# Which engine multiplies the keys by the running products: VectorE for all units in place of GpSimd from the second on

## The chip, the cores and the metric

One core of a Trainium2 chip runs the whole kernel. The metric is device microseconds from start to end of one execution; the median of the runs is what counts. A profiled execution stands beside them, with the time of every instruction of every engine.

## The reference

The kernel computes a linear attention with a state, and then two dense feed-forward layers on its output. For 32 heads (4 batches x 8) of 768 steps, with vectors of 40 elements:

```python
for t in range(S):
    y[:, :, t] = np.einsum('bhd,bhde->bhe', rt, state)
    Sa = np.einsum('bhde,bhe->bhd', state, at)
    state_decay = state * wt[:, :, None, :] - np.einsum('bhd,bhe->bhde', Sa, bt)
    state = state_decay + np.einsum('bhd,bhe->bhde', vt, kt)
```

The 3072 x 320 result goes through h = x @ w_in, a smooth ramp, g @ w_out (320 to 2048 to 320), and a second layer of the same size whose nonlinearity is s * relu(h)^2 + b. The weights of both layers come as float64.

## The kernel before, in words

**The attention** is cut into 24 chunks of 32 steps, and two chunks make a unit: 12 units. Within a chunk the decays w become running products. `prep_a` (line 428) makes what a unit needs before the state is known:

- `products_from_right` (L375) scans suf, the running products from the right end of each chunk, and `products_from_left` (L383 a reciprocal, L384 a scan) makes pre, those from the left. Both are VectorE, and both scan in place.
- L445 multiplies ekb (the k and b vectors, 104 x 1024 elements for each of two) by suf. The last one sets the flag kbm, and `stage_k` sends ekb to the tile tk, part of it through DRAM.
- L454 multiplies XA (the a vectors, four instructions of 40 x 512 elements) by pre. XA is a ring of four chunks, and `loads_a` refills a chunk's place after TensorE has used it for xp.
- L466 multiplies XA and ekb on TensorE into ap; L473 (ScalarE) and L474 (VectorE) copy it to am, and SyncE writes am to DRAM (a_scr). Then L484 (VectorE) puts the masked half back into XA by transposes.

`inverse` (line 547) reads a_scr back as la, and inverts triangles of 16 x 16 in steps on VectorE: L566 makes tmp, L569 subtracts it from ln, each step needing the one before. The result goes to DRAM (l_scr). `mend` loads it as lt and completes it to 32 x 32 on TensorE (L598 pl, L609 pq). `chain_a` and `chain_s` then carry the state from chunk to chunk (xp L709, up L724, sp L747, and on VectorE xr = sp x pc, L759), and `chain_b` makes the output of a chunk (tq, tp, gg, py), with the mask of gg on VectorE (L827).

**The first layer** works on 256 tokens (one unit) at a time, as soon as they are there: fin (L954), a nonlinearity on ScalarE and VectorE (`post`, L919 to L922), a split of g into a high and a low part (L932 on ScalarE, L934 on GpSimd), and fout (L985). What isn't done beside the attention is done after it. The second layer (L964, L1003) comes last and works on 512 tokens at a time. GpSimd also converts weights (L238, L327, L330; the first layer's early, the second's after the attention) and clears tiles (L313).

**The order of the work** is not left to a compiler. Each of the functions named is a generator that yields operations with an engine and an estimated duration, and waits for flags or buffers. `Order.run` (line 146) simulates them as threads: it gives each engine the operation that can begin first, the due time (`DUE`, `STEP`) deciding among those close to each other, and issues the instructions in that order. Each engine then runs its instructions strictly in the order issued, with semaphores between engines. The durations it counts with are:

```python
def dve(n, fn, also=False, two=False):
    return Op("DVE", 70 + n / 0.96, fn, also=also, port=two)
...
def pool(n, fn, also=False, rate=2.1):
    return Op("POOL", 150 + n * rate, fn, 170, also=also, port=n > 16)
```

An operation with `port` set can't be planned beside another one with it; `dve2` is `dve` with `two` set. So the order is planned with 2300 ns for an ekb multiplication on GpSimd and 1137 ns on VectorE, and 1225 ns and 603 ns for one of xa.

Buffers that hold a unit's suf, pre and ekb (es, ew, ekb) are single, and am takes the place of pre; so the next unit's pre is loaded when L484 has read am.

Of the kernel before, what the change touches and what calls it, by code (L numbers as in the profile page):

```python
# [33 lines left out]
NS = 8  # L34
FIRST = 300
LOAD = 0.5
LIGHT = 1
SOON = 0
HOT, LEAD = -59.0, 100

# [157 lines left out]
def pe(dur, fn, share=0.0, spare=False):  # L198

    op = Op("PE", dur, fn, 197)  # L200
    op.small, op.share, op.spare = share > 0, share or 0.95, spare
    return op


def dve(n, fn, also=False, two=False):

    return Op("DVE", 70 + n / 0.96, fn, also=also, port=two)
# [6 lines left out]
def act(n, fn, also=False, more=0):  # L214
    return Op("ACT", 60 + n / 1.2 + more, fn, also=also)
# [6 lines left out]
def dma(nbytes, fn, count=1, flag=None, each=475):  # L222

    op = Op("SP", each * count, fn, 980, flag, nbytes / 360)
    op.count = count
    return op
# [22 lines left out]
def fast_path(ctx, tc, inside, ws_em, wp_em, a_em, kb_em, v_em, r_em, v_tok, eye, mask_a, mask_g, eye_kb,  # L249
              w1_in, w1_out, w2_in, w2_out, sb, out):  # L250
    nc = tc.nc
# [117 lines left out]
    def products_from_right(suf):  # L369

        back = lambda t: flat(t)[:, ::-1]
        for h in range(0, 2 * NP, NS):
            a = slice(h, min(h + NS, 2 * NP))
            n = a.stop - h
            yield dve2(2 * n * 33, lambda: nc.vector.tensor_tensor_scan(out=back(suf[:, a]), data0=back(suf[:, a]), data1=back(start_s[:, 0:n]), initial=1.0,  # L375
                                                                    op0=ALU.mult, op1=ALU.add), h > 0)

    def products_from_left(suf, pre):

        for h in range(0, 2 * NP, NS):  # L380
            a = slice(h, min(h + NS, 2 * NP))
            n = a.stop - h
            yield dve(50, lambda: nc.vector.reciprocal(out=start_p[:, 0:n, 0], in_=suf[:, a, 0]))  # L383
            yield dve2(2 * n * 32, lambda: nc.vector.tensor_tensor_scan(out=flat(pre[:, a]), data0=flat(pre[:, a]), data1=flat(start_p[:, 0:n]), initial=0.0,  # L384
                                                                    op0=ALU.mult, op1=ALU.add))
# [42 lines left out]
    def prep_a():  # L428
        for u in range(NU):
            yield due("prep", u)  # L430
            mk, eng = (dve2, nc.vector) if u < 1 else (pool, nc.gpsimd)
            yield Wait(("start", 1))
            yield Wait(("lw", u + 1))
            suf = sufs[u]
            yield from products_from_right(suf)
            yield act(32, lambda: nc.scalar.copy(out=pc[:, :, 2 * u % 6:2 * u % 6 + 2], in_=suf[:, :, 0].rearrange("p (a c) -> p a c", c=2)))
            yield Wait(("lp", u + 1))
            pre = pres[u]
            yield from products_from_left(suf, pre)
            od.set("pc", 2 * u + 2)  # L440
            od.spawn(stage_e(u, suf, pre), due("stage", u).value)
            yield Wait(("lk", u + 1))
            ekb = ekbs[u]
            for x in range(2):
                yield mk(1024, lambda: eng.tensor_tensor(out=ekb[:, x], in0=ekb[:, x], in1=suf[:, :, 1:C + 1], op=ALU.mult), x > 0)  # L445
            od.set("kbm", u + 1)
            od.spawn(stage_k(u, ekb), due("stage", u).value)
            for c2 in range(2):
                yield Wait(("la", 2 * u + c2 + 1))
                for x in range(2):  # L450
                    r = slice(64 * x, 64 * x + 40)
                    xa = XA[(2 * u + c2) % RING]
                    mk, eng = (pool, nc.gpsimd) if u >= LIGHT else (dve2, nc.vector)
                    yield mk(512, lambda: eng.tensor_tensor(  # L454
                        out=xa[r, x], in0=xa[r, x], in1=pre[r].rearrange("e (p c) t -> e c p t", c=2)[:, c2], op=ALU.mult), x > 0)
            kbv = ekb.rearrange("e y (p c) t -> e c p y t", c=2)
            for c2 in range(2):
                yield Acq("a")
                ap = pa.tile([128, 8, 2, C], F32, tag="a", name="ap")
                xa = XA[(2 * u + c2) % RING]  # L460

                def mm():
                    for m in range(8):
                        for q in range(4):
                            p, x = 8 * (q // 2) + m, q % 2
                            nc.tensor.matmul(ap[32 * q:32 * q + 32, m], lhsT=xa[64 * x:64 * x + 40, x, p, :],  # L466
                                             rhs=kbv[64 * x:64 * x + 40, c2, p], start=True, stop=True, tile_position=(64 * x, 32 * q))

                yield pe(1030, mm, 0.17)
                if c2 == 0:  # L470
                    yield Wait(("ew", u + 1), ("const", 1))
                    am = emp.tile([128, 2, 2, 8, C], F32, tag="ew", name="am")
                yield act(256, lambda: nc.scalar.copy(out=am[:, 1, c2], in_=ap[:, :, 1, :]))  # L473
                yield dve(256, lambda: nc.vector.tensor_tensor(  # L474
                    out=am[:, 0, c2], in0=ap[:, :, 0, :], in1=mska.unsqueeze(1).to_broadcast([128, 8, C]), op=ALU.mult), True)
                od.rel("a")
                if c2 == 1:
                    od.set("ekb", u + 1)
                yield dma(128 * 2048, lambda: nc.sync.dma_start(
                    out=a_scr[u][c2].rearrange("m q t j -> (q t) m j"), in_=am[:, 1, c2]), 1, ("A", 2 * u + c2 + 1))  # L480
            for c2 in range(2):
                for q in range(4):
                    d0 = 0 if q % 2 else 64
                    yield dve(256, lambda: nc.vector.transpose(out=XA[(2 * u + c2) % RING][d0:d0 + 32, q % 2, 8 * (q // 2):8 * (q // 2) + 8, :],  # L484
                                                               in_=am[32 * q:32 * q + 32, 0, c2]), q > 0)
                od.set("XL", 2 * u + c2 + 1)
            od.rel("ew")

    def stage_e(u, suf, pre):

        def put():
            for x in range(2):
                nc.sync.dma_start(out=em_scr[u][x].rearrange("b e n -> e b n"), in_=pre[64 * x:64 * x + 32].rearrange("e (b a) t -> e b (a t)", b=4))
                nc.sync.dma_start(out=et_scr[u][x].rearrange("p e n -> e p n"), in_=pre[64 * x + 32:64 * x + 40].rearrange("e (p c) t -> e p (c t)", c=2))

        yield dma(128 * 3072, put, 4, ("et", u + 1))
        yield Acq("tk")
        tk = att.tile([128, NP, 2, C], F32, tag="tk", name="tk")
        tks[u] = tk, att.tile([128, 4, 2, C], F32, tag="tb", name="tb")
        for i, t in enumerate((pre, suf[:, :, 0:C])):  # L500
            yield act(1176, lambda: nc.scalar.activation(out=tk[0:104].rearrange("p a c t -> p (a c) t"), in_=t, func=AF.Abs,
                                                         accum_out=tot[0:104, 2 * u + i:2 * u + i + 1]))
            if i == 0:
                od.set("ew", u + 1)
        od.set("tot", u + 1)
        yield Wait(("kbm", u + 1))
        od.rel("es")

    def stage_k(u, ekb):

        yield Wait(("tot", u + 1))
        tk, tb = tks[u]

        def put():
            for x in range(2):
                for y in range(2):
                    g = 2 * (1 - x) + y
                    nc.sync.dma_start(out=tk[32 * g:32 * g + 32].rearrange("e p c t -> e (p c t)"), in_=ekb[64 * x:64 * x + 32, y].rearrange("e a t -> e (a t)"))

        def tail():  # L520
            for x in range(2):
                nc.sync.dma_start(out=kt_scr[u][1 - x].rearrange("y h e n -> e (y h) n"),
                                  in_=ekb[64 * x + 32:64 * x + 40].rearrange("e y (h a) t -> e (y h) (a t)", h=4))

        yield dma(128 * 1024, tail, 2, ("kt", u + 1))
        yield dma(128 * 4096, put, 4, ("tk", u + 0.5), 650)
        yield Wait(("kt", u + 1))
        yield dma(128 * 1024, lambda: nc.sync.dma_start(out=tb.rearrange("p i c t -> p (i c t)"), in_=kt_scr[u].rearrange("x y h e n -> (x y h e) n")), 1, ("tk", u + 1))
        yield Wait(("ekb", u + 1), ("tk", u + 1))
        od.rel("ekb")  # L530
# [710 lines left out]
```

## Time and profile before

| | us |
|---|---|
| median of 3 runs | 1236.17 |
| lowest and highest | 1234.88, 1250.49 |
| profiled execution, its own time | 1242.7 |
| its span, first to last instruction | 1240.9 |

Rows name a line (L445), an engine, an operation, and tiles as output<-inputs. The engines are PE (TensorE), PEld (its weight loads), DVE (VectorE), ACT (ScalarE), POOL (GpSimd) and SP (SyncE). A granted clock of 1.00 is TensorE's full 2.4 GHz, 0.50 is 1.2 GHz. The chain of waits follows the work that ended last back to the start, each piece being what released the next; what isn't in it was done early enough.

### The profile page before, as it was taken

The page shows a single profiled execution, that of the slowest core. Times are in us where ns is not written, and L with a number is a line of the kernel's source. Part 1 is how long each engine was busy: PE and PEld are TensorE (multiplying, and loading weights), DVE is VectorE, ACT ScalarE, POOL GpSimd, SP SyncE. Part 2 cuts the span into 40 slices and gives each one's busy share as a digit, 9 for nine tenths or more (in the row PEclk, how much of TensorE's full clock was granted, in tenths as well). Part 3 has the DMA queues.
Part 4 walks back from the last instruction along what each step waited for, and adds up shares of the span by engine and source line. Part 5 has one row for each costly group of instructions (what it writes and reads, how often), then busy time and mean ns, then how long its engine had stood idle before and what let it go on. Part 6 is the DMA issues. An engine that isn't in the chain of part 4 may idle for free.

```text
span 1240.9 us, 47386 instructions
## 1 busy us (share of the span) xinstructions
PE 1125.5 (91%) x20654; PEld 1025.2 (83%) x20654; DVE 736.5 (59%) x1629; ACT 757.4 (61%) x1537; POOL 360.9 (29%) x333
## 2 busy tenths in 40 slices
PE   3897899889898989989899999999999999999995
PEld 3796788778787778878788889999888889888895
DVE  4775877666568676777647343277974344444432
ACT  2433767557476565765666677688765555555553
POOL 5555563414143331323421112366540000000000
PEclk9898699899899988989999999999999999999998
DMA  7875525464555546474432210156201010101000
GB/s 195 239 199 138 125 58 124 91 140 99 110 108 109 124 95 126 81 149 104 96 79 61 44 43 14 34 172 205 69 1 48 1 47 4 45 10 26 16 7 24
DMA packets 188415, 107.36 MB, mean 87 GB/s; under 512 B 149126, under 2 KB 167686, under 8 KB 186950
## 3 DMA queue, kind: packets, MB, share of 16 engines
q1 hardware_dynamic: 188198, 104.24, 35.4%
q8 instruction: 164, 2.69, 0.9%
q14 instruction: 53, 0.43, 0.1%
HBM read 78.25 MB, written 19.66 MB: 79 GB/s over the span
## 4 chain that ended last, share of the span: by engine, by line
PE 72%; DVE 8%; ACT 5%; issue 5%; DMA 5%; SPq 1%; POOL 1%; DVEq 0%; ACTq 0%; POOLq 0%
PE h L954 14%; PE h L964 12%; PE acc L985 12%; PE acc L1003 12%; PE h L1034 6%; PE gg L819 2%; PE sp L747 2%; PE tq L768 2%; PE ap L466 2%; PE py L840 1%; PE xp L709 1%; PE up L724 1%; DMA lt<-lscr 1%; PE tp L802 1%; PE ptx L873 1%
## 5 line engine op out<-in xcount | busy, mean ns | idle before, releaser
L934 POOL TENSOR_TENSOR gl<-g,gh 128x512 fp32r<-128x512 f32 x96 | 125.4, 1306 | 433.9 <-ACT gh L932 380.0
L954 PE MATMUL h<-xh,w 128*128 128x256 f32 x1152 | 228.1, 301 | 5.7 <-DVE g L922 2.9
L954 PEld LDWEIGHTS h<-xh,w 128*128 128x128 f32 x1152 | 182.2, 198 | 12.4 <-issue 3.9
L985 PE MATMUL acc<-w,gh 128*128 128x320 f32 x768 | 190.6, 335 | 0.0
L1003 PE MATMUL acc<-w,gh 128*128 128x320 f32 x768 | 173.1, 312 | 2.6 <-ACT o L1016 2.1
L932 ACT CAST gh<-g 128x512 fp32r<-128x512 f32 x192 | 118.9, 619 | 61.1 <-DVE g L922 37.1
L1003 PEld LDWEIGHTS acc<-w,gh 128*128 128x128 f32 x768 | 132.2, 189 | 11.6 <-ACT o L1016 3.9
L934 DVE TENSOR_TENSOR gl<-g,gh 128x512 fp32r<-128x512 f32 x96 | 68.1, 709 | 117.7 <-ACT gh L932 117.5
L985 PEld LDWEIGHTS acc<-w,gh 128*128 128x128 f32 x768 | 130.9, 198 | 5.0 <-issue 0.2
L985 PE MATMUL acc<-w,gl 128*128 128x320 f32 x384 | 123.0, 320 | 0.0
L1003 PE MATMUL acc<-w,gl 128*128 128x320 f32 x384 | 118.7, 309 | 0.0
L928 ACT ACTIVATE g<-g,sbt 128x512 f32<-128x512 f32 x96 | 78.3, 816 | 64.8 <-DVE g L926 64.7
L954 PE MATMUL h<-xl,w 128*128 128x256 f32 x384 | 111.5, 290 | 0.4 <-issue 0.4
L922 DVE SCALAR_TENSOR_TENSOR g<-h,g 128x512 f32<-128x512 f32 x96 | 66.1, 688 | 75.1 <-ACT h L921 46.4
L919 ACT ACTIVATE g<-h,sbt 128x512 f32<-128x512 f32 x96 | 65.9, 687 | 64.8 <-PE h L954 61.7
L926 DVE SCALAR_TENSOR_TENSOR g<-h,g 128x512 f32<-128x512 f32 x96 | 66.3, 691 | 60.7 <-ACT g L925 60.6
L925 ACT ACTIVATE g<-h 128x512 f32<-128x512 f32 x96 | 57.2, 596 | 72.1 <-PE h L964 72.1
L1034 PE MATMUL h<-w 128*128 128x256 f32 x668 | 91.5, 299 | 0.0
L1034 PEld LDWEIGHTS h<-w 128*128 128x128 f32 x668 | 87.1, 204 | 1.4 <-issue 0.3
L238 POOL TENSOR_TENSOR t<-t,w 128x384 int32<-128x384 int32 x64 | 67.6, 1060 | 68.3 <-DVE t L236 41.0
L759 DVE TENSOR_TENSOR xr<-sp,pc 40x320 f32<-40x320 f32 x92 | 44.8, 487 | 58.4 <-PE sp L747 56.9
L964 PE MATMUL h<-xx,w 128*128 128x512 f32 x288 | 76.8, 402 | 2.1 <-DVE w L330 2.1
(107 smaller groups left out, 2277.7 us busy)
## 6 DMA issues: line engine op xcount, KB each, us to landing
w<-in_w_in SPq DMA_DIRECT2D x32, 384.0 KB
w<-in_w_out SPq DMA_DIRECT2D x32, 320.0 KB
ekb<-in_kb_em SPq DMA_DIRECT2D x12, 832.0 KB
tk<-ekb SPq DMA_DIRECT2D x48, 128.0 KB
suf<-in_ws_em SPq DMA_DIRECT2D x12, 429.0 KB
pre<-in_wp_em SPq DMA_DIRECT2D x12, 416.0 KB
xa<-in_a_em SPq DMA_DIRECT2D x48, 80.0 KB
xr<-in_v_tok SPq DMA_DIRECT2D x48, 80.0 KB
```

The source lines that it names most:

```text
L238: (pool, n, lambda: nc.gpsimd.tensor_tensor(out=t, in0=t, in1=lo, op=ALU.add)),
L919: yield act(512, lambda: nc.scalar.activation(out=g, in_=h, func=AF.Relu, bias=sbt[:, 2:3]), more=93)
L922: yield dve(512, lambda: nc.vector.scalar_tensor_tensor(out=g, in0=h, scalar=1.0, in1=g, op0=ALU.subtract, op1=ALU.add))
L926: yield dve(512, lambda: nc.vector.scalar_tensor_tensor(out=g, in0=h, scalar=0.0, in1=g, op0=ALU.max, op1=ALU.mult))
L928: yield act(512, lambda: nc.scalar.activation(out=g, in_=g, func=AF.Identity, scale=sbt[:, 0:1], bias=sbt[:, 1:2]), more=230)
L932: yield act(512, lambda: nc.scalar.copy(out=gh, in_=g))
L934: yield mk(512, lambda: eng.tensor_tensor(out=gl, in0=g, in1=gh.bitcast(F32), op=ALU.subtract))
L954: yield pe(8 * 118, lambda: [nc.tensor.matmul(h[:, i, :], lhsT=a, rhs=b, start=m == 0, stop=m == 7) for m, (a, b) in enumerate(mm)])
L964: yield pe(4 * 224, lambda: [nc.tensor.matmul(h, lhsT=a, rhs=b, start=4 * i + m == 0, stop=4 * i + m == 7) for m, (a, b) in enumerate(mm[4 ...
L985: yield pe(6 * 147, lambda: [nc.tensor.matmul(acc[0, n][u], lhsT=a, rhs=b, start=p == 0 and m == 0, stop=p == NFF // 2 - 1 and m == 5) for ...
L1003: yield pe(3 * 147, lambda: [nc.tensor.matmul(acc[1, n][u], lhsT=a, rhs=b, start=f == 0 and m == 0, stop=f == NFF - 1 and m == 2) for m, ( ...
L1034: yield pe(2 * 109, lambda: [nc.tensor.matmul(h[:, i, :], lhsT=wh[:, 0:128], rhs=wh[:, 0:256], start=True, stop=True) for i in range(2)], ...
```

## The change

In `prep_a` the engine of the multiplications at L445 (ekb by suf) and L454 (xa by pre) is VectorE for all 12 units, where GpSimd did them from the second unit on. The constant LIGHT, the first unit on GpSimd, falls away. The planner counts with VectorE's durations for them.

```diff
-LIGHT = 1
...
     def prep_a():
         for u in range(NU):
             yield due("prep", u)
-            mk, eng = (dve2, nc.vector) if u < 1 else (pool, nc.gpsimd)
+            mk, eng = dve2, nc.vector
             yield Wait(("start", 1))
...
                     xa = XA[(2 * u + c2) % RING]
-                    mk, eng = (pool, nc.gpsimd) if u >= LIGHT else (dve2, nc.vector)
+                    mk, eng = dve2, nc.vector
                     yield mk(512, lambda: eng.tensor_tensor(
```

## Rows read from the trace of the kernel before

**Rows 1.** The page, busy time (share of the span), and the chain by engine.
```profile
PE 1125.5 (91%) x20654; PEld 1025.2 (83%) x20654; DVE 736.5 (59%) x1629; ACT 757.4 (61%) x1537; POOL 360.9 (29%) x333
...
PE 72%; DVE 8%; ACT 5%; issue 5%; DMA 5%; SPq 1%; POOL 1%; DVEq 0%; ACTq 0%; POOLq 0%
```

**Rows 2.** Windows: length, busy us (instructions) of each engine, granted clock, DMA.
```profile
55.00:640.00 585.00, 517.64 (x14138) 468.24 (x14138) 409.46 (x1021) 350.28 (x781) 227.03 (x189) 0.90 0.52 115
...
100.00:200.00 100.00, 83.58 (x2376) 74.89 (x2376) 67.67 (x167) 64.33 (x152) 56.95 (x55) 0.81 0.47 103
400.00:500.00 100.00, 89.42 (x2685) 79.52 (x2689) 65.38 (x173) 57.74 (x129) 27.94 (x24) 0.86 0.54 115
1000.00:1100.00 100.00, 99.71 (x558) 89.53 (x557) 41.44 (x68) 57.92 (x95) 0.00 (x0) 1.00 0.10 25
```

**Rows 3.** The chain of waits in order of time: start us, us, what.
```profile
214.70 6.70 DMA lt<-lscr
...
397.46 2.13 DVE tmp L566
...
513.03 2.00 DVE ln L569
515.03 2.62 DVE pre L384
...
555.00 1.86 DVE tmp L566
561.05 2.02 DVE ln L569
...
594.72 2.42 DMA lt<-lscr
...
606.35 1.95 DVE ln L569
```

**Rows 4.** The tile ekb: ns shortest/median/longest, first and last start.
```profile
L445 POOL TENSOR_TENSOR ekb<-ekb,suf x22: 2152/2189/2661, 58.5 to 613.6; 104x1024 f32<-104x1024 f32 x22
...
L445 DVE TENSOR_TENSOR ekb<-ekb,suf x2: 1211/1624/2037, 15.0 to 17.0; 104x1024 f32<-104x1024 f32 x2
```

**Rows 5.** The tile xa, the same view.
```profile
L454 POOL TENSOR_TENSOR xa<-xa,pre x44: 1255/1276/1302, 64.2 to 632.5; 40x512 f32<-40x512 f32 x44
...
L454 DVE TENSOR_TENSOR xa<-xa,pre x4: 673/682/690, 18.1 to 20.7; 40x512 f32<-40x512 f32 x4
```

**Rows 6.** The tiles ln and pre, the same view.
```profile
L566 DVE TENSOR_TENSOR tmp<-ln,la x180: 135/241/2134, 53.4 to 676.6; 128x15 f32<-128x15 f32 x24, 128x28 f32<-128x28 f32 x24, 128x39 f32<-128x39 f32 x24, 128x48 f32<-128x48 f32 x24
L569 DVE TENSOR_TENSOR ln<-ln,tmp x180: 140/207/2124, 54.8 to 677.2; 128x15 f32<-128x15 f32 x24, 128x28 f32<-128x28 f32 x24, 128x39 f32<-128x39 f32 x24, 128x48 f32<-128x48 f32 x24
...
L384 DVE TENSOR_TENSOR_SCAN pre<-pre,start_p x48: 650/685/2719, 7.8 to 610.2; 104x256 f32<-104x256 f32 x48
```

**Rows 7.** Windows of multiplications on GpSimd: length, VectorE busy (instructions), clock, DMA.
```profile
224.46:228.77 4.31, 1.44 (x2) 0.50 0.67 87
301.70:305.67 3.97, 0.98 (x2) 1.00 0.62 142
512.75:517.10 4.35, 4.35 (x4) 1.00 0.02 4
```

**Rows 8.** The timeline of VectorE: start us, us, instruction [idle before <-releaser].
```profile
58.99 2.12 DVE L569 TENSOR_TENSOR ln<-ln,tmp 128x39 f32<-128x39 f32 x1
...
304.08 0.99 DVE L759 TENSOR_TENSOR xr<-sp,pc 40x320 f32<-40x320 f32 x2 [6.54 <-PE sp L747]
...
512.95 2.08 DVE L569 TENSOR_TENSOR ln<-ln,tmp 128x64 f32<-128x64 f32 x1
514.96 2.70 DVE L384 TENSOR_TENSOR_SCAN pre<-pre,start_p 104x256 f32<-104x256 f32 x1
...
606.28 2.02 DVE L569 TENSOR_TENSOR ln<-ln,tmp 128x28 f32<-128x28 f32 x1
```

**Rows 9.** Waits on GpSimd: us in total, times, longest.
```profile
POOL xa L454 <- DMA xa<-in_a_em: 7.7, 4, 2.9
```

## The prediction

> **What bounds the kernel now.** I read the page first, then the windows, the chain of waits, and at last the views of the two tiles. On the page TensorE is busy 91% of the span, VectorE 59%, GpSimd 29%, and TensorE holds 72% of the chain that ended last, VectorE 8%, GpSimd 1% [rows 1]. The reader is to see that this average hides two stages. From 1000 to 1100 us TensorE is busy 99.71 of 100 us at a granted clock of 1.00: the second MoE layer is pure TensorE work and nothing in this change touches it. From 55 to 640 us, where the attention units 1 to 11 are prepared and carried through, it is busy 517.64 of 585 us, so 67 us are idle, and the mean granted clock is 0.90; VectorE is busy 409.46 us (70%) and GpSimd 227.03 us (39%) [rows 2]. The end moves only by what the change does to those 67 idle us and to the clock there: matmul work is the same, and what isn't done beside the attention is done after it.
>
> The chain of waits in that stage says what makes TensorE wait. Four times it stands on the landing of lt, the triangular inverse on its way back from DRAM (16.6 us in all; first and last piece shown), and in other places it runs through VectorE's scans of pre and the steps of the inverse (tmp and ln) [rows 3]. Neither L445 nor L454 on GpSimd holds a single piece of the chain between 55 and 660 us. So the multiplications are hidden as durations; what can be felt is how they stand in VectorE's way.
>
> **What the change removes.** GpSimd loses 22 ekb instructions of 2189 ns (median) and 44 xa instructions of 1276 ns [rows 4, 5]: 48.2 + 56.1 = 104 us, 9.5 us for each of 11 units. GpSimd has idle time anyway, so that gives nothing by itself. But six pieces of the chain are VectorE instructions that ran much longer than usual: 2.13, 2.00, 2.62, 1.86, 2.02 and 1.95 us [rows 3], where a step of the inverse has a median of 241 or 207 ns and a scan one of 685 ns [rows 6]. Each lies in the shade of an ekb multiplication; the instruction at 512.95 us (2.08 us) and the one at 514.96 us (2.70 us) show it, as the two ekb multiplications run from 512.75 us for 4.35 us [rows 7, 8]. Such an instruction counts as busy but stands until GpSimd is done. I went through VectorE's timeline for all 22 + 44 multiplications and took the usual duration off each VectorE instruction beside them: 16 are stretched by ekb, 28.0 us in all, and 11 by xa, 8.0 us; the first is the one of 2.12 us at 58.99 us, the last large one that of 2.02 us at 606.28 us [rows 8]. So 36 us of VectorE's busy time go. On the chain, the six pieces sum to 12.6 us; at usual durations (five steps at about 0.2, one scan at 0.69) they would take 1.7 us, so 10.9 us go there.
>
> VectorE instructions that read PSUM aren't stretched: the pair of L759 at 304.08 us, inside three xa multiplications that run from 301.70 us for 3.97 us, took 0.99 us, 0.5 us each [rows 7, 8]. These ran beside GpSimd and will stand behind VectorE's own multiplications: the change takes away a lock on some instructions and puts a queue in front of all.
>
> The Trainium skill, page "SBUF — State Buffer", section "SBUF: two separate sides", has this as a rule: a GpSimd instruction and a VectorE instruction with two SBUF inputs (or in a two-port mode) exclude each other for the whole instruction, whichever started first. By that rule all 104 us are closed to such instructions, and if VectorE had always had one ready, the change would take 104 us off and not 36. The trace agrees with the mechanism (2.70 us against 0.69), but in the windows of the multiplications VectorE was busy from 4.35 of 4.35 us down to 1.44 of 4.31 [rows 7], so the 36 us counted are used.
>
> **What it adds.** VectorE gets the 22 ekb and 44 xa instructions. Unit 0 runs them there already: ekb took 1.21 us at the least and 1.62 us in the median of two, of which one was held up; xa 0.68 us [rows 4, 5]. So 22 x 1.21 to 1.62 = 26.6 to 35.7 us, and 44 x 0.682 = 30.0 us: 57 to 66 us, 5.1 to 6 us for each unit. The spread stays because GpSimd keeps some 120 us in the stage (227 - 104), beside which the new instructions may be held up in turn. I take 61 us.
>
> It also moves waits. On GpSimd xa waited four times for its DMA, 7.7 us in all, the longest 2.9 us [rows 9]. GpSimd could afford this; on VectorE, which issues in order, everything behind waits too: steps of the inverse, xr = sp x pc for the chain, the masks of gg. Bounds: 0, if the hand-made order puts xa where the load has landed, and 7.7 us or more, if it doesn't. I take 7.7 us. No DMA is added or removed, but the ones behind kbm and XL (tk, kt, am to DRAM) are issued from SyncE's queue at other times.
>
> **The sum.** VectorE: +61 + 7.7 - 36 = +33 us in 585, three us for each unit, so that its busy share goes from 70% to 75%. How much reaches the end? On the page VectorE holds 8% of the span's chain and is busy 59%: about one us in seven counts (0.135). That gives +4.4 us. The second way goes by pieces: -10.9 us; 6 of the 22 ekb were felt before, and if as many are felt at 1.21 to 1.62 us that is +7 to +10; xa and its waits at 0.135 of 37.7 us is +5.1. Together +1 to +4. I take +4.
>
> The preparation itself gets shorter: 2 x 2.19 + 4 x 1.28 = 9.5 us become 2 x 1.42 + 4 x 0.68 = 5.6 us. Bounds: nothing, as no piece of the chain is one of these multiplications, and the 16.6 us that the chain stands on lt, if an earlier xa brings an earlier inverse. The loop from xa over ap, A and inverse to lt goes through four transfers and the thirty steps of an inverse, and one piece on lt alone is up to 6.70 us [rows 3]; so I take nothing.
>
> Last, the order. Every engine's order is written by the list scheduler in Order.run, with 2300 and 1225 ns for the two GpSimd instructions and 1137 and 603 ns on VectorE. With other costs on another engine the whole order from unit 1 on is another one. Its price has no row; the nearest is the clock: 0.81 from 100 to 200 us, 0.86 from 400 to 500, 0.90 over the stage [rows 2]. A stretch of 100 us at 0.81 and not 0.90 costs 9 us of TensorE's time, one at 0.90 and not 0.81 gives that back. I take +1 and keep 9 us either way for the range. In all +5 us: by the profiled execution's own time, 1242.7 us, 1247.7; the median of the runs shown is 6.5 us under it, so 1236.2 + 5 = **1241 us**, no difference that a measurement of this kernel could tell from none (it can tell about 2%, 25 us).
>
> **The rivals.**
> *VectorE becomes the bound of the attention stage (slower).* Place: the inverse of unit u, thirty dependent steps on VectorE, between which the list scheduler puts whatever else is ready, now six multiplications of unit u + 1. For it: the inverse is what lt waits for, and the inverse's steps and scans are VectorE's pieces on the chain. Against: VectorE idles 175 us of the 585. It decides if the added time is felt in full, not at one in seven: +33 us, 1269 us; above 0.75 felt it is 25 us and past 2%.
> *The lock goes and the stage tightens (faster).* For it: six stretched pieces on the chain, 10.9 us, and 16.6 us of waits for lt; if VectorE's idle time takes in the new work, both go: -27 us, 1209 us. Against: these waits have their length from DMA and from the order as well, and other waits come late next.
> *All of it lies beside TensorE's work.* Neither lock nor added work is felt: 1236 us. For it: 86% of the chain isn't VectorE's or GpSimd's. Against: the six pieces.
> The Trainium skill, page "Perfetto Trace Analysis", section "Optimizing Scalar/DVE Operations", warns that moving operations between these two engines might not help, as they share a port; that would be this last case, and the stretched rows are what speaks against it being all.
>
> **How the numbers follow.** Chances: the forecast 0.48, with a range of its own of 1226 to 1257 (the clock's 9 us and the bounds of the DMA wait and of ekb); the slower rival 0.27, the faster one 0.13, no effect 0.12. The range goes from 1214, near the faster rival, to 1272, the slower one with 3 us beyond its price; under and over it lie about 0.1 each. Faster by over 2% means under 1211.5 us: most of the faster rival at its full price, 0.09. Slower by over 2% means over 1260.9 us: most of the slower rival, 0.24. The rest is 0.67.
>
> **What would show it.** Right: no GpSimd row for L445 and L454; VectorE ekb near 1.2 to 1.6 us x24 and xa near 0.68 us x48; the maximum of scans and of inverse steps down from 2.7 and 2.1 us to that of other GpSimd instructions (about 1.3 us); VectorE busy some 20 to 30 us more; TensorE busy from 55 to 640 us within 10 us of before. Wrong: the units run closer together or further apart by over 2 us each, with more or less time on lt in the chain, or a granted clock in the stage that is off 0.90 by over 0.03.

## The result, and the profile after

The changed kernel takes 1221.26 us (median of 12 runs, 1217.52 to 1231.22); the kernel before took 1238.76 us beside it (12 runs). The ratio is 0.985, with an interval of 0.983 to 0.988: faster by 1.5%, some 18 us. The forecast was slower by 5 us; its own range, 1226 to 1257 us, misses the result, the wide one (1214 to 1272) holds it. The profiled execution took 1219.44 us with a span of 1217.6, so the two profiles differ by 23 us, 6 us more than the medians. The ratios are formed from the faster runs of both kernels (those over 1.5% above a kernel's fastest are left out), so they can differ a little from the quotient of medians. Lines stand one lower than before (L445 is L444), as LIGHT is gone.

The page of the changed kernel: busy time, and the filler matmuls that TensorE runs until the first layer can begin; the third line is the one of the fillers before:

```profile
PE 1106.8 (91%) x20532; PEld 1003.7 (82%) x20532; DVE 763.6 (63%) x1695; ACT 757.3 (62%) x1537; POOL 265.2 (22%) x267
...
L1033 PE MATMUL h<-w 128*128 128x256 f32 x546 | 79.4, 309 | 0.0
...
L1034 PE MATMUL h<-w 128*128 128x256 f32 x668 | 91.5, 299 | 0.0
```

Beside [rows 1]: VectorE has 27 us more, GpSimd 96 us less. TensorE has 19 us less. 12 us of it are fillers: the first layer's first block begins at 146.4 us and not at 162.0. The other 7 us are the same 19986 matmuls done in less time, at a mean granted clock of 0.954 for 0.943 over the span. TensorE's idle time falls by 5 us (110.8 for 115.4). As fillers stand where TensorE would wait, some 17 of the 23 us are waiting that went, and 7 are matmuls that ran faster.

The window of the attention stage, columns as in [rows 2]:

```profile
55.00:640.00 585.00, 523.25 (x14775) 468.64 (x14775) 452.09 (x1125) 368.33 (x819) 133.24 (x128) 0.92 0.54 118
```

In the same 585 us TensorE now issues 14775 matmuls, 637 more, at a clock of 0.92 for 0.90. The stage as a whole has moved forward: more of everybody's work falls into the window, VectorE's too.

The tiles ekb, xa, ln and pre of the changed kernel, beside [rows 4 to 6]:

```profile
L444 DVE TENSOR_TENSOR ekb<-ekb,suf x24: 1208/1217/2315, 15.0 to 598.9; 104x1024 f32<-104x1024 f32 x24
...
L453 DVE TENSOR_TENSOR xa<-xa,pre x48: 672/689/1746, 18.1 to 621.5; 40x512 f32<-40x512 f32 x48
...
L565 DVE TENSOR_TENSOR tmp<-ln,la x180: 127/240/1389, 53.4 to 650.2; 128x15 f32<-128x15 f32 x24, 128x28 f32<-128x28 f32 x24, 128x39 f32<-128x39 f32 x24, 128x48 f32<-128x48 f32 x24
L568 DVE TENSOR_TENSOR ln<-ln,tmp x180: 132/207/1285, 54.6 to 650.5; 128x15 f32<-128x15 f32 x24, 128x28 f32<-128x28 f32 x24, 128x39 f32<-128x39 f32 x24, 128x48 f32<-128x48 f32 x24
...
L383 DVE TENSOR_TENSOR_SCAN pre<-pre,start_p x48: 671/686/1367, 7.8 to 596.9; 104x256 f32<-104x256 f32 x48
```

The median durations are those that unit 0 had before. The longest step of the inverse falls from 2.1 to 1.3 or 1.4 us, the longest scan from 2.7 to 1.4. A *hold* is here the time for which a VectorE instruction stands, counted as busy, while one of GpSimd runs. What is left are holds by GpSimd's other instructions: the longest step, 1.39 us at 606.53 us, stands beside one of gl (L933) that runs from 606.51 us for 1.29. The last step of the last inverse starts at 650.5 us and not at 677.2.

The timeline shows the start of it. In the kernel before, VectorE at the end of the first inverse, and GpSimd (POOL) beside it:

```profile
94.03 0.69 DVE L384 TENSOR_TENSOR_SCAN pre<-pre,start_p 104x256 f32<-104x256 f32 x1 [4.22 <-DMA w<-in_w_in]
...
97.15 2.11 DVE L569 TENSOR_TENSOR ln<-ln,tmp 128x15 f32<-128x15 f32 x1
...
96.56 5.12 POOL L445 TENSOR_TENSOR ekb<-ekb,suf 104x1024 f32<-104x1024 f32 x2
```

and in the changed kernel:

```profile
86.54 0.90 DVE L568 TENSOR_TENSOR ln<-ln,tmp 128x15 f32<-128x15 f32 x1
...
87.69 0.68 DVE L383 TENSOR_TENSOR_SCAN pre<-pre,start_p 104x256 f32<-104x256 f32 x1
```

The last step of the inverse starts at 86.54 us and not at 97.15. Two things are to be seen. That step took 2.11 us beside two ekb multiplications of unit 2; a step takes some 0.2 us in the median. And a scan of unit 2, for which VectorE stood idle for 4.22 us, lay in the middle of the inverse before; now it comes behind the inverse's end: the order of issue is another one. (The profile names a load of weights as what the scan waited for; the load of its own data was issued only at 89.66 us.) So there are two candidates, the hold and the order, and the experiments part them.

### The profile page after: what moved, and what is told of

Its sections match the earlier page's. It is cut to its first block, busy times and chain, and to the rows that moved or that the text cites. A ratio compares the mean times of both kernels' runs of the same rounds, so it can differ in the third digit from the quotient of the medians.

```text
span 1217.6 us, 47095 instructions
## 1 busy us (share of the span) xinstructions
PE 1106.8 (91%) x20532; PEld 1003.7 (82%) x20532; DVE 763.6 (63%) x1695; ACT 757.3 (62%) x1537; POOL 265.2 (22%) x267
## 5 line engine op out<-in xcount | busy, mean ns | idle before, releaser
L933 POOL TENSOR_TENSOR gl<-g,gh 128x512 fp32r<-128x512 f32 x96 | 129.6, 1350 | 524.9 <-ACT gh L931 490.9
L953 PE MATMUL h<-xh,w 128*128 128x256 f32 x1152 | 222.8, 296 | 5.9 <-DVE g L921 3.8
L953 PEld LDWEIGHTS h<-xh,w 128*128 128x128 f32 x1152 | 177.4, 192 | 10.2 <-DVE g L921 4.2
L933 DVE TENSOR_TENSOR gl<-g,gh 128x512 fp32r<-128x512 f32 x96 | 66.8, 696 | 122.1 <-ACT gh L931 121.9
L1002 PEld LDWEIGHTS acc<-w,gh 128*128 128x128 f32 x768 | 131.7, 188 | 11.1 <-ACT o L1015 3.1
L984 PEld LDWEIGHTS acc<-w,gh 128*128 128x128 f32 x768 | 128.6, 195 | 8.1 <-issue 3.0
L237 POOL TENSOR_TENSOR t<-t,w 128x384 int32<-128x384 int32 x64 | 70.3, 1102 | 71.6 <-DVE t L235 43.9
L1033 PE MATMUL h<-w 128*128 128x256 f32 x546 | 79.4, 309 | 0.0
L1033 PEld LDWEIGHTS h<-w 128*128 128x128 f32 x546 | 75.4, 215 | 1.3 <-issue 0.3
L953 PEld LDWEIGHTS h<-xl,w 128*128 128x128 f32 x384 | 74.2, 193 | 2.3 <-issue 2.0
```

Source lines behind the costliest of these rows:

```text
L237: (pool, n, lambda: nc.gpsimd.tensor_tensor(out=t, in0=t, in1=lo, op=ALU.add)),
L933: yield mk(512, lambda: eng.tensor_tensor(out=gl, in0=g, in1=gh.bitcast(F32), op=ALU.subtract))
L953: yield pe(8 * 118, lambda: [nc.tensor.matmul(h[:, i, :], lhsT=a, rhs=b, start=m == 0, stop=m == 7) for m, (a, b) in enumerate(mm)])
L984: yield pe(6 * 147, lambda: [nc.tensor.matmul(acc[0, n][u], lhsT=a, rhs=b, start=p == 0 and m == 0, stop=p == NFF // 2 - 1 and m == 5) for ...
L1002: yield pe(3 * 147, lambda: [nc.tensor.matmul(acc[1, n][u], lhsT=a, rhs=b, start=f == 0 and m == 0, stop=f == NFF - 1 and m == 2) for m, ( ...
L1033: yield pe(2 * 109, lambda: [nc.tensor.matmul(h[:, i, :], lhsT=wh[:, 0:128], rhs=wh[:, 0:256], start=True, stop=True) for i in range(2)], ...
```

## The experiments

The runs were on several chips, and the kernel before ran beside each with medians from 1233.31 to 1245.46 us; so ratios to the kernel before of the same chip are compared, with intervals of some 0.003 to 0.007 either way.

### Engine and order, one at a time

The planner's word for an operation (`pool`, `dve2`) sets the order, the engine in the instruction sets who does it. So each can be changed alone.

```diff
  order_before_on_dve
-            mk, eng = (dve2, nc.vector) if u < 1 else (pool, nc.gpsimd)
+            mk, eng = (dve2, nc.vector) if u < 1 else (pool, nc.vector)
  order_after_on_pool
-            mk, eng = (dve2, nc.vector) if u < 1 else (pool, nc.gpsimd)
+            mk, eng = (dve2, nc.vector) if u < 1 else (dve2, nc.gpsimd)
```

and the same for xa.

> The order of issue is that of the kernel before (the planner counts GpSimd's engine and durations for the multiplications from unit 1 on), but VectorE executes them. Theory A, the lock: what the change gave (17.5 us, ratio 0.985) comes from GpSimd no longer holding up VectorE, so most of it is here, 10 to 18 us under before. Theory B, the order: it comes from the planner's new order, so this is within 4 us of before, or slower by up to 10 us, since VectorE gets 5 us more of each unit at places that weren't planned for it.

Measured: 0.989 (0.983 to 0.995), which is 13.8 us of that chip's 1244.59; the medians themselves are 9.5 us apart.

> The order of issue is that of the changed kernel (the planner counts VectorE's durations and VectorE as the engine), but GpSimd executes the multiplications from unit 1 on. Theory A, the lock: the stretched steps come back, so the time is that of before or above, 0 to +15 us. Theory B, the order: 10 to 18 us under before, as in the changed kernel.

Measured: 0.992 (0.989 to 0.996). Neither theory stands alone: the engine gives 1.1% in the old order, the new order 0.8% with GpSimd still at work. From there to the changed kernel (0.985) the engine gives 0.7% in the new order. The order gives 0.4% with VectorE, which the intervals don't tell from nothing.

What the engine does is seen in the tile ln of order_after_on_pool, beside the one of the changed kernel above, whose order it has:

```profile
L566 DVE TENSOR_TENSOR tmp<-ln,la x180: 130/242/2229, 52.9 to 663.9; 128x15 f32<-128x15 f32 x24, 128x28 f32<-128x28 f32 x24, 128x39 f32<-128x39 f32 x24, 128x48 f32<-128x48 f32 x24
L569 DVE TENSOR_TENSOR ln<-ln,tmp x180: 123/212/5205, 53.6 to 664.1; 128x15 f32<-128x15 f32 x24, 128x28 f32<-128x28 f32 x24, 128x39 f32<-128x39 f32 x24, 128x48 f32<-128x48 f32 x24
```

The long steps are back, and the last one starts at 664.1 us for 650.5.

### One of the two, and one of the units

ekb_only and xa_only take one of the two lines of the diff; unit1_only has `u < 2` for ekb and LIGHT = 2; all_but_unit1 has GpSimd for `u == 1` alone.

> Only the 22 ekb multiplications go to VectorE, planned and executed there; xa stays on GpSimd. Theory A, the lock: ekb carried 28 of the 36 us of stretching and all six stretched pieces of the chain, so this gives most, 9 to 15 us under before. Rival, the latency of the preparation: xa stands last before ap, and its four multiplications are 5.1 of the 9.5 us; then ekb alone gives half or less, 3 to 8 us.

> Only the 44 xa multiplications go to VectorE, planned and executed there; ekb stays on GpSimd. Theory A, the lock: 8 of 36 us of stretching, so 0 to 5 us under before. Rival, the latency: 8 to 14 us under before. If both single moves and neither theory fit (both give all, or neither gives any), the order as such is what moves the time.

Measured: ekb_only 0.990 (0.986 to 0.994), 15 us by the medians; xa_only 0.999 (0.995 to 1.002). That is as the holds were counted (28 us of stretching for ekb, 8 for xa) and against the latency of the preparation as the reason. But each of the two edits also writes an order of its own, so alone they don't show it.

> Both multiplications go to VectorE for unit 1 alone (with unit 0, as before); units 2 to 11 keep GpSimd. Theory S, the start: in the changed kernel the first inverse ends 11 us earlier (86 for 97 us) and the first layer's first block starts 16 us earlier, so unit 1 alone gives 8 to 15 us and the rest adds little. Rival, every unit: the gain is one of 1 to 2 us for each unit, so unit 1 alone gives 0 to 3 us.

> The other half: unit 1 keeps GpSimd, units 2 to 11 go to VectorE. Theory S, the start: 0 to 5 us under before. Rival, every unit: 12 to 17 us under before.

Measured: unit1_only 0.999 (0.995 to 1.002), all_but_unit1 1.002 (0.998 to 1.006). Both theories are wrong: neither part gives anything, and together they give 1.5%. unit1_only does have the early start, with 592 fillers for 668, and loses it again on the way. So parts don't add up, as is to be expected if each edit rewrites the order from the second unit to the last; the next runs test that.

### How much an order is worth

```diff
  planned_as_measured (GpSimd)
-                yield mk(1024, lambda: eng.tensor_tensor(out=ekb[:, x], ...
+                yield Op("POOL", 2189, lambda: eng.tensor_tensor(out=ekb[:, x], ...
  after_as_measured (VectorE)
-                yield mk(1024, lambda: eng.tensor_tensor(out=ekb[:, x], ...
+                yield Op("DVE", 1217, lambda: eng.tensor_tensor(out=ekb[:, x], ...
```

and so for xa; after_less and after_more have other numbers in the second.

> A control: GpSimd executes all, as in the kernel before, and only the planner's durations for the two are set to what the trace shows (2189 for 2300 ns, 1276 for 1225 ns). Nothing that a theory speaks of is changed. If the order as such is worth little, this is within 4 us of before; if any small change of the plan moves the time by some 10 us, it is off by that, either way, and then gains of that size in single runs say little of their cause.

Measured: 0.993 (0.989 to 0.996). Some 4 to 5% on two planned durations, no engine changed, and the kernel is faster by 0.7%.

> A control on the changed kernel: VectorE executes all, and only the planner's durations for the two are set to what the trace of the changed kernel shows (1217 for 1137 ns, 689 for 603 ns). If the order of the changed kernel is one among many, this falls anywhere from 0.980 to 1.000 of before; if VectorE as the engine is what makes the order good, it stays at 0.982 to 0.989.

Measured: 0.975 (0.969 to 0.980), 1214.18 us beside 1245.46: clear of the changed kernel's 0.985. A truer plan could be the reason, so the error was made larger (1057 and 517 ns) and turned around (1297 and 775 ns):

> The changed kernel with the planner's durations set as far below its own as after_as_measured has them above (1057 and 517 ns; its own are 1137 and 603, the trace shows 1217 and 689). If a truer plan is what made after_as_measured faster, this is slower than the changed kernel, 0.990 to 1.000 of before. If orders differ by luck, it is anywhere from 0.975 to 1.000.

> The changed kernel with the planner's durations above those of the trace (1297 and 775 ns). If a truer plan is what counts, or one with some room, this stays near after_as_measured, 0.972 to 0.982 of before; if luck, anywhere from 0.975 to 1.000.

Measured: after_less 0.977 (0.972 to 0.982), after_more 0.993 (0.990 to 0.997). A truer plan isn't it: a plan twice as far off as the changed kernel's (160 ns too short for ekb, where that one's is 80) is as good as the true one, and one that is 80 ns too long isn't. Four orders with all the multiplications on VectorE, planned there, with only these durations apart, lie at 0.975, 0.977, 0.985 and 0.993: a spread of 1.9%, more than the change under study.

The window of the attention stage in after_as_measured, and in after_more:

```profile
55.00:640.00 585.00, 523.38 (x14623) 471.64 (x14623) 443.38 (x1117) 369.00 (x823) 133.36 (x127) 0.94 0.54 118
```

```profile
55.00:640.00 585.00, 518.53 (x14218) 466.70 (x14220) 435.71 (x1089) 354.80 (x790) 125.96 (x123) 0.89 0.53 116
```

Good and poor order differ in this stage: 14623 matmuls at a clock of 0.94 against 14218 at 0.89, with 5 us between them in TensorE's busy time.

### The engine in further orders

> The same order of issue as in planned_as_measured (which came out at 0.993 of before), but VectorE executes the multiplications from unit 1 on. Theory A+B (the lock is worth about 0.7 to 1.1% in any order, and an order by itself some 1% either way): the lock comes off this order as well, so 0.982 to 0.988 of before. Rival, only the order counts: 0.990 to 0.996, as with GpSimd in that order.

Measured: 0.993 (0.990 to 0.997), the same as with GpSimd in that order.

> The same order of issue as in all_but_unit1 (1.002 of before, with VectorE from unit 2 on), but GpSimd executes the multiplications of all units from 1 on. If that order is a poor one and the lock is worth 0.7 to 1.1% in it too, this is 1.006 to 1.014 of before. If the lock is worth nothing there, it is 0.998 to 1.006, as with VectorE.

Measured: 1.018 (1.012 to 1.023), against 1.002 with VectorE from unit 2 on. So all_but_unit1 showed no gain because its order is a poor one; VectorE wins 1.5% back in it.

> The order of issue of after_as_measured (0.975 of before, with VectorE), but GpSimd executes the multiplications from unit 1 on: a fifth order with both engines. By the four before, where GpSimd cost 0.0, 0.7, 1.1 and 1.6% against VectorE in one order, this is 0.975 to 0.991 of before, and more likely near 0.983. If it is above 0.991, GpSimd costs more where the order is tight.

Measured: 0.988 (0.983 to 0.993), against 0.975 with VectorE.

| order of issue of | on GpSimd | on VectorE | VectorE to GpSimd |
|---|---|---|---|
| the kernel before | 1.000 | 0.989 | 0.989 |
| the changed kernel | 0.992 | 0.985 | 0.993 |
| planned_as_measured | 0.993 | 0.993 | 1.000 |
| all_but_unit1 (unit 1 on GpSimd in both) | 1.018 | 1.002 | 0.985 |
| after_as_measured | 0.988 | 0.975 | 0.986 |

With the order held, VectorE is never slower; the five pairs have a mean of 0.991, some 11 us, and go from nothing to 1.5%. Four of the five are clear of the noise.

These pairs change two things: the hold goes, and the multiplications get shorter. The chain of waits tells which counts. Its shares by engine in after_as_measured_on_pool, then in after_as_measured, and the first and last of VectorE's pieces over 2 us in the former:

```profile
PE 67%; DVE 13%; issue 7%; DMA 6%; ACT 4%; SPq 2%; POOL 1%; DVEq 0%; ACTq 0%; POOLq 0%
...
PE 74%; DMA 6%; DVE 6%; issue 6%; ACT 3%; SPq 2%; POOL 1%; DVEq 0%; ACTq 0%; POOLq 0%
...
154.53 2.61 DVE pre L384
...
620.90 2.62 DVE pre L384
```

With GpSimd eight scans and steps of the inverse stand on the chain with 2.0 to 2.6 us each, 18 us in all, each beside an ekb multiplication; no multiplication on GpSimd is itself a piece of it between 50 and 700 us. With VectorE in the same order none of VectorE's pieces there is over 1.3 us for one instruction. The old order says the same: the six long pieces of [rows 3] are gone in order_before_on_dve. So what counts in these two orders is the hold, and not the multiplications' own length. One order doesn't fit: planned_as_measured has five such pieces on its chain (11 us), and VectorE gains nothing in it. The chain of measured_on_dve can't be followed back into the stage, so the reason stays open.

### The hold without the work, and one step further

In cut_on_pool GpSimd keeps the multiplications in the old order, but from unit 1 on each works on 1 of 32 columns, so 31 of 32 columns of ekb and xa stay unmultiplied.

```diff
+                n = 1 if u else C
-                yield mk(1024, lambda: eng.tensor_tensor(out=ekb[:, x], in0=ekb[:, x], in1=suf[:, :, 1:C + 1], op=ALU.mult), x > 0)
+                yield mk(1024, lambda: eng.tensor_tensor(out=ekb[:, x, :, 0:n], in0=ekb[:, x, :, 0:n], in1=suf[:, :, 1:n + 1], op=ALU.mult), x > 0)
```

and so for xa.

> The order of the kernel before, the multiplications on GpSimd, but from unit 1 on each works on 1 of 32 columns, so it leaves out nearly all of that multiplying. That takes GpSimd's hold off VectorE and gives VectorE nothing in its place. Theory A, the lock: at least as much as with VectorE in the same order (13.8 us under before), by up to 8 us more. If VectorE's added 56 us cost nothing, both are equal.

Measured: 0.993 (0.990 to 0.997), while VectorE doing all of the work in that order has 0.989 (0.983 to 0.995). The tile ekb, the busy time of the page, and the window of the stage:

```profile
L446 POOL TENSOR_TENSOR ekb<-ekb,suf x22: 292/310/775, 58.6 to 598.8; 104x32 f32<-104x32 f32 x22
...
PE 1120.3 (92%) x20654; PEld 1019.9 (83%) x20654; DVE 700.7 (57%) x1629; ACT 757.8 (62%) x1537; POOL 274.1 (22%) x333
...
55.00:640.00 585.00, 528.93 (x14590) 477.28 (x14589) 377.01 (x1030) 363.09 (x810) 142.60 (x193) 0.92 0.53 117
```

and the same window of order_before_on_dve:

```profile
55.00:640.00 585.00, 519.38 (x14326) 469.67 (x14324) 431.43 (x1088) 356.01 (x793) 126.71 (x123) 0.92 0.53 116
```

VectorE's busy time on the page falls by 36 us against the kernel before (700.7 for 736.5), with the same 1629 instructions: that is the 36 us of stretching that the prediction counted.

54 us more on VectorE in the stage (431 for 377) cost nothing that can be measured; by the two intervals it can be at most about 4 us. The chain of order_before_on_dve says how much of it is felt:

```profile
447.33 1.22 DVE ekb L445
...
453.89 0.69 DVE xa L454
```

Two of the 22 ekb and two of the 44 xa stand on it, 4.0 us in all with some crumbs. VectorE's idle time takes in the rest. (Some hold is left in cut_on_pool, as its 66 short instructions still run on GpSimd.)

The last one moves further instructions of GpSimd that hold VectorE, those of gl, to VectorE:

```diff
  after_gl_on_dve (on the changed kernel, in post)
-        mk, eng = (dve2, nc.vector) if l else (pool, nc.gpsimd)
+        mk, eng = dve2, nc.vector
```

> The changed kernel, and the first layer's split of g (96 instructions of 128 x 512) goes from GpSimd to VectorE as well. If VectorE gains by every hold of GpSimd that goes, 0.975 to 0.985 of before. If VectorE is full by then (452 of 585 us before this, 96 x 0.70 us more), 0.990 to 1.010.

Measured: 1.002 (0.999 to 1.006), 1.7% worse than the changed kernel. In a single order that can be VectorE's load or a poor order; it wasn't taken apart.

## Why the prediction was wrong

**What bounds the kernel** was read rightly: the second layer is untouched, and the gain is made before it, while the attention runs. The matmuls done there rose, and the clock from 0.90 to 0.92, within the 0.03 that the prediction allowed. TensorE's busy time there moved by 6 us, as forecast.

**What is removed** was right, in kind and size. The stretched steps went, and the pieces of the chain were put at -10.9 us; cut_on_pool, where nearly all of the hold goes, measured 0.7% (8 us), and the five pairs have a mean of 11 us. That VectorE's maxima beside its medians find a hold is shown. The chain of waits gave its price in two orders (the old one and after_as_measured) and not in planned_as_measured; that the mean meets -10.9 so closely is luck, as single orders lie between nothing and 1.5%.

**What is added** is the step that failed: "That gives +4.4 us" and, in the second way, +7 to +10 for ekb and +5.1 for xa. The instructions were sized rightly (1217 and 689 ns in the median, 27 us more for VectorE in all, as 20 to 30 had been said), but they were charged at VectorE's average share of the chain, though VectorE idled 175 of 585 us. On the chain these two charges came to +12 to +15 us; in order_before_on_dve the multiplications hold 4.0 us of it, two ekb in place of six. And cut_on_pool (next to no added work) and order_before_on_dve (all of it) don't differ beyond the noise. The waits for xa's DMA, put at 7.7 us, don't appear in the changed kernel's waits at all. With nothing to 4 us in the place of these terms the second way gives -11 to -7 us: faster, and not slower.

**The order** is the second failure, of size: "I take +1 and keep 9 us either way". Four orders with the same engines lie 1.9% apart, 23 us, so the term is about as large as all others, and it wasn't to be had from the trace. In this change it gave 0.8% (10 us) with GpSimd; with VectorE 0.4%, which isn't clear of the noise.

**The earlier inverse**, taken as nothing, stays open in part. The changed kernel's first inverse does end 12 us earlier and saves fillers, but unit1_only has both and gains nothing, and xa_only, which shortens the last step before ap, gives nothing either.

**The rivals.** The slower one said that VectorE becomes the bound through the inverse; the last inverse ended 26 us earlier. The faster one, with a chance of 0.13, had the right mechanism in its first half, that the lock goes and VectorE's idle time takes in the work; its -27 us was too much by half. Its second half, that the 16.6 us of waits for lt go too, isn't shown: in order_before_on_dve the chain stands on lt for 21.3 us, and that of the changed kernel can't be followed back into the stage. The list's sign of being wrong, units closer together by over 2 us, didn't appear: of the 26 us 12 are there at the end of the first inverse already, and the 11 distances between shrink by 1.3 us each. The signs listed for being right came out, and yet the time was off: none of them could tell the terms of the sum apart. The third rival, no effect, put 86% of the chain outside VectorE and GpSimd; by [rows 1] it is about 90%, and the gain came all the same.

The Trainium skill (page "Perfetto Trace Analysis", section "Optimizing Scalar/DVE Operations") warns that moving operations between these two engines might not help. The runs agree where GpSimd is the place of work: its 104 us of multiplications, though hidden beside everything, cost 0.9% against VectorE on the mean of five orders. They don't agree for the way back to VectorE, which did help.

What stays open is which places of an order make it good.

## What to carry to other kernels

Work on GpSimd isn't free just because GpSimd has idle time: look at the longest duration of VectorE's SBUF instructions beside the median, and price what stands on the chain. Here, work moved to VectorE cost little, as VectorE idled 175 us of the stage. Where a planner writes the order, an edit changes two things: run the new order with the old engine and the old order with the new engine before the gain is credited to either. And measure the spread of orders with a change of the plan that means nothing; here it is 1.9%. The best of such orders (0.975, with planned durations of 1217 and 689 ns) is 1.1% faster than the changed kernel.

## What the runs showed of the hardware that was not expected

An instruction with one SBUF input is held as well. In the kernel before, one L235 (a shift of 128 x 320 integers, 0.27 us when free, as at 59.06 us in the changed kernel) took 2.25 us, beside the second of two ekb multiplications that run from 58.48 to 63.21 us:

```profile
61.15 2.25 DVE L235 TENSOR_SCALAR t<-w 128x320 int32<-128x320 int32 x1
```

And a hold can span several GpSimd instructions. In order_after_on_pool one step of the inverse took 5.2 us, longer than any GpSimd instruction there (2.66 us for the longest ekb). It stood from 100.47 us through the rest of an ekb multiplication, a weight conversion, one of xa and another conversion, that is until 105.7 us. Before, no VectorE instruction in the tiles looked at had been over 2.72 us.

```profile
100.47 5.21 DVE L569 TENSOR_TENSOR ln<-ln,tmp 128x15 f32<-128x15 f32 x1
```
